# A text gate spread over its rows by eight transfers inside SBUF, in an image-and-text attention block on one core

## The chip, the cores and the metric

The kernel runs on one core of a Trainium2 chip. The metric is device time in microseconds (us) of one launch. Three runs of the kernel before took 117.28, 117.15 and 116.58 us, median 117.15. All positions in time below are from one profiled execution, counted from the start of its span.

Engine names are those of the profile: PE is TensorE's matmuls and PEld its weight loads, DVE is VectorE, ACT is ScalarE, POOL is GpSimd, SP is SyncE. SPq, ACTq and POOLq are the queues on which these engines issue DMA transfers.

## The reference

Two batches of 256 image tokens and 32 text tokens with 1152 features go through one block of joint attention. The part that matters is the end of it:

```python
mod_t = (_silu(c) @ wmod_txt).reshape(B, 6, 1, D)
...
sht, sct, gat = mod_t[:, 0], mod_t[:, 1], mod_t[:, 2]
...
a = softmax(q @ k.T * D ** -0.5) @ v          # text and image tokens together
at, ai = a[:, :Nt], a[:, Nt:]
out_i = x_img + gai * (ai @ wo_img)
out_t = x_txt + gat * (at @ wo_txt)
```

`gat` is the text gate: one row of 1152 numbers for each batch. Every one of a batch's 32 text rows of `at @ wo_txt` is multiplied by it, element by element, before `x_txt` is added. `gai` is the same for the image.

## The kernel before

The kernel is one long program for five engines with one order of instructions for each, written out by hand: the scheduler is set to manual, so an engine's instructions stand in the order in which the Python code emits them, and a wait at the head of an engine's queue holds everything behind it. Tiles come out of pools with a fixed number of buffers, used in turn; a tile that takes over a buffer waits for the last reader of the tile before it. PSUM has seven such buffers under one tag (`mm`), each one bank.

It loads 14 blocks of weights on SyncE's queue one after the other, and TensorE works through them: the image's modulation and V, then Q and K for the image (line 459), the text's Q and K (line 518), scores and softmax, the attention product (line 682), and last the output products. Only this last stage is touched by the change.

**Image output.** The 512 image rows are four tiles of 128; each tile's 1152 output columns are made in three chunks of 384 (`out_chunk`). A chunk is nine matmuls on TensorE (line 773), a VectorE multiply by the image gate out of PSUM (line 779) and a VectorE add of `x_img` (line 780). The last chunk of the last tile is cut into 256 and 128 columns; its weights are gated beforehand by GpSimd (line 757), so that VectorE only has to add (line 776). Tiles 0 to 2 are stored in one transfer each on SyncE's queue (line 784), tile 3 piece by piece, the piece of 256 columns on ScalarE's queue and the others on SyncE's (line 782).

**Text output.** The 64 text rows are few for 128 partitions, so the 1152 columns are laid out as two halves r of two groups g of 288 columns: text row t of batch b stands, for group g, in partition 64 g + 32 b + t, and half r is a second stretch along the row. `out_txt_mm` makes both halves in two PSUM tiles (`ops`) with 72 matmuls (line 794).

**Text gate.** `txt_gate` calls `mod_rows`: 36 matmuls (line 432) that leave in one PSUM tile `gps`, for quarter q = 2 r + g of the columns, batch b's gate in row 32 q + b. The tile is copied to SBUF as bf16 (`g_sb`, 288 columns) by `evac`, a helper that takes VectorE and ScalarE in turn and here takes VectorE (line 151). Only eight of its 128 rows hold gate values.

**Spreading.** Each text row needs its gate in its own partition. `txt_gate_spread` does that with two matmuls (line 747), one for each half r: the weights are `selF`, a 0/1 matrix that picks row 32 (2 r + g) + b for each of the 32 rows of (g, b); the result (`bps`) is copied by ScalarE to `gbf` (line 749). `selF` is made early, by eight small copies on GpSimd (line 333).

**Text end.** `out_txt_end` takes each half through a VectorE multiply by `gbf` (line 803) and an add of `x_txt` (line 804), then stores the two groups, one on SyncE's and one on ScalarE's queue (line 807).

The order in which these are emitted at the end is: tiles 0 and 1, tile 2's first two chunks, text gate, text products, spreading, text end, tile 2's last chunk, tile 3.

## Time and profile before

| What | Value |
|---|---|
| Median of three runs (lowest, highest) | 117.15 us (116.58, 117.28) |
| The profiled execution's own time | 116.77 us |
| Its span in the profile | 114.7 us |
| TensorE busy | 110.0 us, 96% |
| VectorE busy | 53.6 us, 47% |
| ScalarE busy | 34.1 us, 30% |
| GpSimd busy | 25.0 us, 22% |
| Granted TensorE clock | full in all 40 slices |

The span is the stretch from the first to the last instruction in the trace; the profiled execution's own time is 2.0 us longer. Busy shares are averages over stages with different limits, so what a change is worth is read from the stage in which it lies. The chain that ended last follows the work back from the last instruction, at each step to what released it. In a row of a group or of the timeline stand the line, the engine, the operation, the tile written and the tile read, the shapes, how many, and then busy time, mean length and what the engine waited for; matmul rows overlap, since they are pipelined, so the distance from one start to the next says more than the length of one. In the rows by half microseconds stand the stretch, its length, the busy time of PE, PEld, DVE, ACT and POOL with the number of instructions, the granted clock, the busy share of the DMA engines and GB/s. A row of a DMA issue names the transfer, its size, and the time from the start of its issue to its landing.

### The profile page before, as it was taken

How to read it: one execution, taken by the hardware profiler on the slowest of the kernel's cores; microseconds unless marked ns; L12 is line 12 of the kernel's file. 1: busy time of each engine (PE TensorE's matmuls, PEld its weight loads, DVE VectorE, ACT ScalarE, POOL GpSimd, SP SyncE). 2: the span in 40 equal slices, each digit the busy share in tenths (PEclk: the TensorE clock that was granted, in tenths of full speed). 3: DMA queues.
4: the chain of work that ended last, by engine and by line, in shares of the span. 5: the costliest groups of instructions: out<-in, count | busy, mean ns of one | idle time of the engine just before them, and what ended most of it. 6: DMA issues, size and time to landing. Idle time of an engine off the chain costs nothing.

```text
span 114.7 us, 2951 instructions
## 1 busy us (share of the span) xinstructions
PE 110.0 (96%) x1264; PEld 65.6 (57%) x1264; DVE 53.6 (47%) x139; ACT 34.1 (30%) x83; POOL 25.0 (22%) x56
## 2 busy tenths in 40 slices
PE   5998999999999999999999999999999999999990
PEld 1354664544944444486444546987677565567670
DVE  1798820452470402211752432137656805994771
ACT  2829660343360321021270122115455700000200
POOL 7000102560140000003233000000340301998000
PEclk9999999999999999999999999999999999999999
DMA  3999999999999999999999999999999999961052
GB/s 116 297 319 352 369 384 400 412 413 411 410 404 404 411 412 405 410 411 415 401 411 411 392 412 409 407 415 401 411 405 405 405 419 408 407 244 70 6 189 69
DMA packets 22872, 40.89 MB, mean 356 GB/s; under 512 B 1215, under 2 KB 6731, under 8 KB 22859
## 3 DMA queue, kind: packets, MB, share of 16 engines
q1 hardware_dynamic: 22000, 39.82, 91.0%
q0 software_dynamic: 480, 0.73, 1.7%
q10 hardware_dynamic: 379, 0.14, 0.5%
q8 instruction: 10, 0.16, 0.5%
q14 instruction: 3, 0.02, 0.1%
HBM read 39.36 MB, written 1.34 MB: 355 GB/s over the span
## 4 chain that ended last, share of the span: by engine, by line
PE 87%; DMA 6%; SPq 2%; DVE 2%; issue 0%
PE qkps L459 31%; PE ps L773 15%; PE va L242 11%; DMA x_i<-in_x_img_dram 6%; PE aps L682 5%; PE ps L518 4%; PE sps L542 4%; PE gps L370 4%; PE ops L794 2%; PE ps L346 2%; PE ps L397 2%; PE ps L614 2%; SPq L93 2%; PE mps L202 1%; PE gps L432 1%; PE tp L185 1%
## 5 line engine op out<-in xcount | busy, mean ns | idle before, releaser
L459 PE MATMUL qkps<-hT_i,t 128*128 128x512 bf16 x162 | 35.6, 379 | 0.0
L459 PEld LDWEIGHTS <-t 128*128 128x128 bf16 x162 | 15.6, 98 | 18.3
L773 PE MATMUL ps<-t,aT 128*128 128x384 bf16 x99 | 16.4, 326 | 0.0
L773 PEld LDWEIGHTS <-aT 128*128 128x128 bf16 x117 | 11.1, 98 | 6.7 <-issue 0.2
L242 PE MATMUL va<-w_v_i,hT_i 128*128 128x512 bf16 x63 | 14.5, 379 | 0.3 <-DMA w_v_i<-in_wqkv_img_dram 0.3
L757 POOL TENSOR_TENSOR w_og<-t,gb 128x384 bf16<-128x384 bf16 x9 | 8.7, 997 | 5.9 <-DMA t<-in_wo_txt_dram 5.9
L242 PEld LDWEIGHTS <-hT_i 128*128 128x128 bf16 x63 | 5.8, 97 | 7.0 <-ACT hT_i L190 0.6
L779 DVE TENSOR_TENSOR tmp<-ps,gb 128x384 bf16<-128x384 f32 x11 | 6.0, 549 | 4.8 <-DMA gb<-mod_scratch 4.0
L443 DVE TENSOR_SCALAR qkT<-qkps 128x512 bf16<-128x512 f32 x4 | 2.8, 692 | 11.6 <-PE qkps L459 11.6
L137 PE MATMUL wps<-wz 128*128 128x512 bf16 x16 | 6.2, 546 | 1.2 <-DVE wz L127 1.2
L160 DVE BATCH_NORM_STATS2 stats<-x_i 128x6 f32<-128x384 bf16 x12 | 5.9, 544 | 2.7 <-DMA x_i<-in_x_img_dram 2.7
L445 ACT ACTIVATE qkT<-qkps 128x512 bf16<-128x512 f32 x5 | 2.9, 596 | 13.5 <-PE qkps L459 13.5
L151 DVE CAST qkT<-qkps 128x512 bf16<-128x512 f32 x4 | 2.8, 692 | 7.2 <-PE qkps L459 7.2
L226 POOL TENSOR_SCALAR hT_i<-hT_i,mod_img 128x256 bf16<-128x256 bf16 x5 | 2.5, 510 | 15.7 <-ACT rstd L167 9.0
L153 ACT CAST qkT<-qkps 128x512 bf16<-128x512 f32 x5 | 2.8, 587 | 10.3 <-PE qkps L459 10.3
L569 POOL DMA_DIRECT2D mod_scratch<-g_sb x2 | 1.2, 583 | 20.9 <-ACT g_sb L567 20.9
L780 DVE TENSOR_TENSOR o<-tmp,x_i 128x384 bf16<-128x384 bf16 x11 | 5.2, 473 | 0.4
L695 DVE TENSOR_SCALAR aT<-aps,sv 128x288 bf16<-128x288 f32 (+2 forms) x11 | 4.3, 454 | 2.2 <-PE aps L682 2.2
L518 PEld LDWEIGHTS <-t 128*128 128x128 bf16 x162 | 4.9, 98 | 0.2
L749 ACT CAST gbf_full<-bps 128x288 bf16<-128x288 f32 x2 | 0.7, 402 | 14.2 <-PE bps L747 14.2
L518 PE MATMUL ps<-hT_t,t 128*128 128x64 bf16 x162 | 4.9, 193 | 0.0
L682 PE MATMUL aps<-pT,v_i 128*128 128x288 bf16 (+2 forms) x44 | 4.8, 264 | 0.1
(157 smaller groups left out, 141.2 us busy)
## 6 DMA issues: line engine op xcount, KB each, us to landing
t<-in_wmod_txt_dram SPq DMA_DIRECT2D x3, 2592.0 KB, 22.0
t<-in_wmod_img_dram SPq DMA_DIRECT2D x2, 2592.0 KB, 22.4
t<-in_wqkv_img_dram SPq DMA_DIRECT2D x6, 864.0 KB, 14.1
t<-in_wqkv_txt_dram SPq DMA_DIRECT2D x2, 2592.0 KB, 17.4
t<-in_wqkv_txt_dram SPq DMA_DIRECT2D x3, 864.0 KB, 14.2
t<-in_wo_img_dram SPq DMA_DIRECT2D x1, 2592.0 KB
t<-in_wo_txt_dram SPq DMA_DIRECT2D x3, 864.0 KB, 15.0
w_v_i<-in_wqkv_img_dram SPq DMA_DIRECT2D x4, 576.0 KB, 7.8
```

The lines of the kernel that those rows point to most:

```text
L137: nc.tensor.matmul(ps[:], lhsT=wz[:, 0:P], rhs=wz[:], start=True, stop=True)
L160: nc.vector.bn_stats(stats[0:np_, k, :], x_ap[:, k * CH:(k + 1) * CH])
L242: nc.tensor.matmul(ps[:], lhsT=hT_i[:, kt, i * P:(i + 1) * P], rhs=w_v_i[:, kt, half * VW:(half + 1) * VW], start=(kt == 0), stop=(kt == K ...
L370: nc.tensor.matmul(gps[32 * g:32 * g + 32, 0:RC], lhsT=lhs[:, kt, :], rhs=wt[:, kt, g * RC:(g + 1) * RC], start=(kt == 0), stop=(kt == KT ...
L459: nc.tensor.matmul(pss[j - j0][:], lhsT=wq[:, kt, j * P:(j + 1) * P], rhs=hT_i[:, kt, :], start=(kt == 0), stop=(kt == KT - 1))
L518: nc.tensor.matmul(ps[:, j - j0, :], lhsT=wq[:, kt, j * P:(j + 1) * P], rhs=hT_t[:, kt, :], start=(kt == 0), stop=(kt == KT - 1))
L542: nc.tensor.matmul(sps[:], lhsT=qkT[:, ft, b, q0:q0 + P], rhs=qkT[:, KT + ft, b, :], start=(ft == 0), stop=(ft == KT - 1))
L682: nc.tensor.matmul(bank[:, off:off + c1 - c0], lhsT=lhsT, rhs=rhs, start=(first[id(bank)] == n), stop=(final[id(bank)] == n))
L757: nc.gpsimd.tensor_mul(w_og[:, dt, 0:CH], w_o_i[:, dt, NG0:D], gb[:, B - 1, NG0:D])
L773: nc.tensor.matmul(ps[:, 0:cw], lhsT=aT[:, dt, t0:t0 + P], rhs=rhs, start=(dt == DTS[0]), stop=(dt == DTS[-1]))
L779: nc.vector.tensor_mul(tmp[:, 0:cw], ps[:, 0:cw], gb[:, b, cs])
L780: nc.vector.tensor_add(o[:, cs], tmp[:, 0:cw], x_i[:, i, cs])
```

## The change

The selection matrix `selF` and its eight GpSimd copies go. `mod_rows` copies the gate rows to SBUF on ScalarE, by name, where `evac` chose VectorE. The spreading is done without TensorE and ScalarE's copies: for each batch b, half r and group g, one transfer reads row 32 (2 r + g) + b of `g_sb` 32 times and writes the 32 partitions from 64 g + 32 b on of `gbf`. The four transfers of batch 0 are issued on SyncE's queue, those of batch 1 on ScalarE's. And the order at the end is another: the spreading is issued right behind the gate products and ahead of the text products, and the text end stands behind tile 2's last chunk instead of ahead of it. The text products, the text end's own instructions and all image chunks are the same.

```diff
-    selF = const.tile([P, 2, 2, B, NT], bf)
-    for r in range(2):
-        for g in range(2):
-            for b in range(B):
-                col = 32 * (2 * r + g) + b
-                nc.gpsimd.tensor_copy(selF[:, r, g, b, :], ident[:, col:col + 1].to_broadcast([P, NT]))
...
-        evac(g_sb[:, 0:VC], gps[:])
+        nc.scalar.copy(g_sb[:, 0:VC], gps[:])
...
     def txt_gate_spread(g_sb):
-        for r in range(2):
-            bps = ps_mm.tile([P, VC], f32, tag="mm")
-            nc.tensor.matmul(bps[:], lhsT=selF[:, r, :, :, :].rearrange("p g b t -> p (g b t)"), rhs=g_sb[:, 0:VC],
-                             start=True, stop=True)
-            nc.scalar.copy(gbf[:, r, :], bps[:])
+        for b in range(B):
+            eng = nc.sync if b == 0 else nc.scalar
+            for r in range(2):
+                for g in range(2):
+                    row = 32 * (2 * r + g) + b
+                    q = 64 * g + NT * b
+                    eng.dma_start(gbf[q:q + NT, r, :], g_sb[row:row + 1, 0:VC].rearrange("p (o j) -> p o j", o=1).to_broadcast([1, NT, VC]))
...
     g_sb = txt_gate()
+    txt_gate_spread(g_sb)
     pss = out_txt_mm()
-    txt_gate_spread(g_sb)
+    out_chunk(2, 2 * CH, CH)
     out_txt_end(pss)
-    out_chunk(2, 2 * CH, CH)
     out_chunk(3, 0, CH, nc.sync)
```

## The prediction

> **What bounds the kernel now.** I read the page first (busy shares, the 40 slices), then the chain that ended last, then the timelines of TensorE and VectorE from 95 us on, last the busy time and the DMA share by half microseconds.

> ```profile
> PE 110.0 (96%) x1264; PEld 65.6 (57%) x1264; DVE 53.6 (47%) x139; ACT 34.1 (30%) x83; POOL 25.0 (22%) x56
> ...
> PE 87%; DMA 6%; SPq 2%; DVE 2%; issue 0%
> ```

> TensorE is busy 96% of the span, and 87% of the chain that ended last is its matmuls. Until about 101 us the weight loads fill the DMA engines too, but the change lies behind them. The chain in order of time, around the change (start, length, what):

> ```profile
> 102.36 1.22 PE gps L432 x36
> 103.58 2.21 PE ops L794 x72
> 105.78 0.35 PE bps L747 x2
> 106.14 5.89 PE ps L773 x45
> 112.02 0.02 issue
> 112.05 0.29 DVE o L776
> ```

> No step here waits for another engine: gate products, text products, the two selection products, then the 45 matmuls of the last five chunks. Only the final VectorE add stands behind them, then store and closing. So time is saved only by taking work off TensorE, and lost only by what comes later than 112.05. VectorE at that end:

> ```profile
> 106.48 0.46 DVE L803 TENSOR_TENSOR tmp<-ops,gbf_full 128x288 bf16<-128x288 f32 x1 [2.02 <-ACT gbf_full L749]
> 106.97 0.31 DVE L804 TENSOR_TENSOR of<-tmp,xf_full 128x288 bf16<-128x288 bf16 x1
> 107.20 0.45 DVE L803 TENSOR_TENSOR tmp<-ops,gbf_full 128x288 bf16<-128x288 f32 x1
> 107.69 0.31 DVE L804 TENSOR_TENSOR of<-tmp,xf_full 128x288 bf16<-128x288 bf16 x1
> 107.91 0.55 DVE L779 TENSOR_TENSOR tmp<-ps,gb 128x384 bf16<-128x384 f32 x1
> 108.50 0.36 DVE L780 TENSOR_TENSOR o<-tmp,x_i 128x384 bf16<-128x384 bf16 x1
> 109.10 0.56 DVE L779 TENSOR_TENSOR tmp<-ps,gb 128x384 bf16<-128x384 f32 x1 [0.24 <-PE ps L773]
> 109.69 0.36 DVE L780 TENSOR_TENSOR o<-tmp,x_i 128x384 bf16<-128x384 bf16 x1
> 110.56 0.56 DVE L779 TENSOR_TENSOR tmp<-ps,gb 128x384 bf16<-128x384 f32 x1 [0.51 <-PE ps L773]
> ```

> The text end (four instructions, 106.48 to 107.91, 1.43 us) runs while TensorE makes tile 2's last chunk, so VectorE has caught up by 109.10 and again by 110.56, with gaps of 0.24 and 0.51 us. That slack, 0.75 us and what is left behind 110.56, is what a later text end uses up.

> **TensorE: two products of 128x288 go.** The chain puts 0.35 us on them. But the weight load in front of them shows a gap of 0.24 us (the arrays change from 32 columns to 128), which the chunk behind will have instead. In the TensorE timeline the first selection product starts at 105.72 and the first matmul of the chunk at 105.97:

> ```profile
> 105.72 0.42 PE L747 MATMUL bps<-g_sb,selF 128*128 128x288 bf16 x2
> 105.97 4.55 PE L773 MATMUL ps<-t,aT 128*128 128x384 bf16 x27
> ```

> So the chunks come 0.25 us earlier (0.35 at most, if the gap goes as well). I take 0.25. TensorE gets no new wait: the spread is off it, and of the seven banks used in turn the chunks get ones read before 104.1.

> **GpSimd: eight copies go**, 1.25 us from 22.2 us on. GpSimd then idles 5.7 us for a VectorE result (line 224), so this is worth nothing.

> **The gate copy goes from VectorE to ScalarE.** VectorE took it at 104.02, between chunks; ScalarE has waited 14.2 us by line 749 and does this shape in 402 ns. Gate products end at 103.58, so the row tile is ready at about 104.02, against 104.47.

> **Eight transfers come**, four from SyncE's queue, four from ScalarE's, each reading one row of 576 bytes 32 times. This trace has none like it. On SyncE they stand behind tile 1's store (issued 102.14) and before tile 2's, which has no data before 108.2; on ScalarE before a text store and the store of a last piece, later still. Each takes over the completion counter of the eighth transfer before it; for the last two those are tiles 0's and 1's stores, and the DMA engines carry nothing from 104.5 on, so neither should hold them. The bus is free:

> ```profile
> 104.50:105.00 0.50, 0.50 (x25) 0.43 (x16) 0.00 (x0) 0.00 (x0) 0.50 (x2) 1.00 0.00 0
> 105.00:105.50 0.50, 0.50 (x28) 0.43 (x16) 0.00 (x0) 0.00 (x0) 0.50 (x1) 1.00 0.00 0
> ```

> The nearest rows are the text stores (the same 576-byte pieces, both queues, an idle bus) and the last small store:

> ```profile
> out_dram<-of SPq DMA_DIRECT2D x1, 72.0 KB, 2.2
> out_dram<-of ACTq DMA_DIRECT2D x1, 72.0 KB, 2.5
> ...
> out_dram<-o SPq DMA_DIRECT2D x1, 32.0 KB, 1.5
> ```

> Issuing took 0.61 to 0.65 us in the text stores, 0.33 in the 32 KB one; with some 0.06 between, one every 0.4 to 0.7 us. From 104.05 the second on each queue (half r=0 complete) starts at 104.45 to 104.75, the fourth (r=1) at 105.25 to 106.15. With 1.5 to 2.5 us to landing: r=0 is there at 105.95 to 107.25, r=1 at 106.75 to 108.65. I take the text stores' row: 107.2 and 108.5.

> **The text end moves behind tile 2's last chunk.** In before the next chunk is taken at 109.10 and the one after at 110.56, 1.46 us apart at TensorE's pace, so tile 2's last chunk was ready at 107.64 and is now at 107.39. A chunk on a VectorE with work waiting takes 0.87 us to the next (95.86 to 96.73, GpSimd idle; 0.98 while GpSimd gates weights, over by 105.7; 0.95 if nothing overlaps). So:
> - chunk 107.39 to 108.26; the text end's first half needs r=0 at 108.26, its second r=1 at 108.98 (0.72 later, as 106.48 to 107.20); both are there, by 1.0 and 0.5 us;
> - text end to 109.69, tile 3's chunks to 110.56 and 111.43 (ready on TensorE at 108.85 and 110.31, so VectorE now sets the pace);
> - the 256 columns: ready 111.29, taken 111.43, 0.42 us at most; the last 128: ready about 111.8, end 112.1.

> Before ended at 112.34. So VectorE just works off its backlog as TensorE ends, and the 0.25 us arrives at the end. With 0.95 a chunk the sum is 112.4: no gain. The two text stores move from 108.02 to 109.7, still 2 us ahead of the last. The four waits in front of the text multiply cost a few hundredths, beside the running add.

> **The sum.** The profiled execution took 116.77 us (span 114.7, 2.0 around it): 116.77 - 0.25 = 116.5. The runs' median is 117.15, 0.4 above it; by that 116.9.

> **Rivals.**

> 1. *The source rows are the bottleneck (slower).* All 147 KB come out of eight rows of SBUF, where every store of this trace reads 64 or 128. If rows lying together give no more than a sixteenth of the full rate (410 GB/s in the slices, so 25.6), the 74 KB of r=0 take 2.9 us: 104.05 + 1.5 + 2.9 = 108.45, 0.2 late. If r=1 goes abreast from 105.0, it lands at about 109.4, 0.4 late: 117.3. If each DMA engine must finish r=0 first, r=1 lands at 111.35, 2.4 late: VectorE stands still and the end moves by 2.4 - 0.25: 119.3. It decides from a landing at 109.2 (gain gone); by 110.4 the kernel is 1% slower. For it: eight rows only. Against it: nothing in the trace reads so few rows at this size.

>    [...]

> 2. *VectorE becomes the bound, transfers hidden.* With 0.95 to 0.98 us a chunk and small costs for waits the end is 112.4 to 112.5: 117.2 to 117.3. For it: five of the seven steps between earlier chunks take 0.98. Against: those run beside GpSimd.

> 3. *The products' removal shows nothing or more.* If TensorE's array change costs more before the wider chunk, the gain is 0; if the gap goes too, 0.35: 116.8 to 117.15. Nothing in the diff can give over 1%, since only 0.35 us leaves the path.

> **How the numbers follow.** Hidden transfers, 116.8 to 117.3 (the forecast, rivals 2 and 3): 0.50. Source rows limiting, halves mostly abreast, 117.3 to 118.3: 0.24. The same in sequence, 118.3 to 119.3: 0.23. Faster by over 1%, only by an effect I do not see: 0.03. One per cent, 1.17 us, is about what a measurement of this kernel can tell from no change; so faster 0.03, same 0.74, slower 0.23. The range runs from 116.5 (forecast less the runs' own scatter of 0.4) to 119.0, leaving the worst of rival 1 out.

> **What would show it.** Right: no selection products, the chunk's first matmul within 0.3 us of the last text product; eight transfers issued from 104.1, landing by 108.5; VectorE without a gap from 107.4 on. Wrong: a wait on a transfer of the gate tile ahead of a text multiply (rival 1; its length is the loss); gaps on VectorE behind the text end would say that I priced the chunks too high.

## The result, and the profile after

The changed kernel took 118.78 us (median of 6 runs, 118.51 to 119.0), beside 117.02 us for the kernel before (also 6 runs). The ratio is 1.0147, with a 95% interval of 1.0122 to 1.0172: **slower by 1.5%**, where the prediction had 116.9 us and no change. Its profiled execution took 118.59 us, with a span of 116.8.

Line numbers of the changed kernel are five to seven lower than before: the transfers are on L744, the chunks on L768, L774 and L775, the text end on L798 and L799. From the page, the busy shares and the shares of the chain:

```profile
PE 109.7 (94%) x1262; PEld 65.3 (56%) x1262; DVE 52.9 (45%) x138; ACT 33.9 (29%) x82; POOL 23.8 (20%) x48
...
PE 79%; DVE 9%; DMA 6%; ACTq 2%; issue 1%; ACT 0%; DVEq 0%
```

The work is smaller on every engine, and the time is longer: 2.1 us of span were added, and TensorE does nothing in them. Its share of the chain that ended last fell from 87% to 79%, and VectorE's rose from 2% to 9%. The chain in order of time shows where TensorE drops out:

```profile
102.42 1.25 PE gps L425 x36
103.67 0.02 issue
103.69 0.41 ACT g_sb L428
104.10 0.02 issue
104.12 0.60 ACTq L744
...
106.33 4.39 DMA gbf_full<-g_sb
...
110.85 0.47 DVE tmp L798
```

In before the products stood in this place without a break. Now the chain leaves TensorE at 103.67, goes through the gate copy and the four issues on ScalarE's queue, and then spends 4.39 us on the last of these transfers. The prediction had that step hidden. VectorE's timeline (start, length, engine, line, operation, shapes, and in brackets what it waited for) says how late it is:

```profile
107.45 0.56 DVE L774 TENSOR_TENSOR tmp<-ps,gb 128x384 bf16<-128x384 f32 x1 [3.25 <-PE ps L768]
108.04 0.36 DVE L775 TENSOR_TENSOR o<-tmp,x_i 128x384 bf16<-128x384 bf16 x1
108.62 0.46 DVE L798 TENSOR_TENSOR tmp<-ops,gbf_full 128x288 bf16<-128x288 f32 x1 [0.22 <-DMA gbf_full<-g_sb]
109.11 0.31 DVE L799 TENSOR_TENSOR of<-tmp,xf_full 128x288 bf16<-128x288 bf16 x1
110.85 0.46 DVE L798 TENSOR_TENSOR tmp<-ops,gbf_full 128x288 bf16<-128x288 f32 x1 [1.43 <-DMA gbf_full<-g_sb]
111.34 0.31 DVE L799 TENSOR_TENSOR of<-tmp,xf_full 128x288 bf16<-128x288 bf16 x1
111.56 0.55 DVE L774 TENSOR_TENSOR tmp<-ps,gb 128x384 bf16<-128x384 f32 x1
...
112.42 0.55 DVE L774 TENSOR_TENSOR tmp<-ps,gb 128x384 bf16<-128x384 f32 x1
...
113.28 0.61 DVE L771 TENSOR_TENSOR o<-ps,x_i 128x256 bf16<-128x256 f32 x2
```

The first text multiply waits 0.22 us for half r=0, the second 1.43 us for half r=1. Behind the second wait stand tile 3's chunks, which TensorE had ready long before (it ends at 111.82), so the last add ends at 113.90. The stage's start differs a little between profiles, since the first loads do; so from here on the end is given as **tail**: the end of the last VectorE add, counted from the first gate product. These are the rows of the first gate product and the last adds in before, and of the first gate product in after:

```profile
102.29 1.29 PE L432 MATMUL gps<-t,sT 128*32 128x288 bf16 x36
111.54 0.80 DVE L776 TENSOR_TENSOR o<-ps,x_i 128x256 bf16<-128x256 f32 x2
```

```profile
102.35 1.29 PE L425 MATMUL gps<-t,sT 128*32 128x288 bf16 x36
```

Before, the tail is 112.34 - 102.29 = 10.05 us; after, it is 113.90 - 102.35 = 11.55.

TensorE itself did what was foreseen. By its timeline the chunk behind the text products starts 3.42 us after the first gate product (105.77 - 102.35), where it was 3.68 in before (105.97 - 102.29):

```profile
103.46 2.38 PE L789 MATMUL ops<-t,aT 128*32 128x288 bf16 x72
105.77 4.56 PE L768 MATMUL ps<-t,aT 128*128 128x384 bf16 x27
```

The transfers, by the rows of DMA issues (queue, size of one, median time from issue to landing) and by half microseconds (the last two columns are the busy share of the DMA engines and GB/s):

```profile
gbf_full<-g_sb SPq DMA_DIRECT2D x4, 18.0 KB, 3.5
gbf_full<-g_sb ACTq DMA_DIRECT2D x4, 18.0 KB, 3.9
out_dram<-of SPq DMA_DIRECT2D x1, 72.0 KB, 2.1
```

```profile
105.50:106.00 0.50, 0.50 (x14) 0.20 (x7) 0.00 (x0) 0.00 (x0) 0.34 (x1) 1.00 0.31 28
106.00:106.50 0.50, 0.50 (x5) 0.31 (x4) 0.00 (x0) 0.00 (x0) 0.00 (x0) 1.00 0.62 28
106.50:107.00 0.50, 0.50 (x5) 0.31 (x4) 0.00 (x0) 0.00 (x0) 0.00 (x0) 1.00 0.74 29
107.00:107.50 0.50, 0.50 (x5) 0.31 (x4) 0.05 (x1) 0.00 (x0) 0.00 (x0) 1.00 0.71 28
107.50:108.00 0.50, 0.50 (x5) 0.30 (x4) 0.50 (x1) 0.00 (x0) 0.00 (x0) 1.00 0.67 65
```

A transfer of 18 KB takes longer to land than a text store of 72 KB. From 105.5 to 107.5, while only half r=0 is read, the DMA engines are up to 74% busy and move 28 GB/s. In the packet records of the trace a 576-byte piece takes mostly 0.21 to 0.25 us from 106 on (median 0.23); pieces of that size took 0.03 to 0.04 us in the text stores. Only when pieces of r=1, which read other rows, come among those of r=0 does the rate double to 65 GB/s.

**A second loss** lies behind the last landing. It takes 0.91 us from there to the end of the span in before (113.83 to 114.74) and 1.28 in after (115.52 to 116.80); this is called the closing below. The tail's 1.50 us and the closing's 0.37 make 1.87, against 1.72 by the ratio (0.0147 of 117.05, interval 1.43 to 2.01).

### The profile page after: what moved, and what is told of

Read it like the earlier page. It is cut to its first block, busy times and chain, and to the rows that moved or that the text cites. A ratio compares the mean times of both kernels' runs of the same rounds, so it can differ in the third digit from the quotient of the medians.

```text
span 116.8 us, 2950 instructions
## 1 busy us (share of the span) xinstructions
PE 109.7 (94%) x1262; PEld 65.3 (56%) x1262; DVE 52.9 (45%) x138; ACT 33.9 (29%) x82; POOL 23.8 (20%) x48
## 4 chain that ended last, share of the span: by engine, by line
PE 79%; DVE 9%; DMA 6%; ACTq 2%; issue 1%; ACT 0%; DVEq 0%
PE qkps L452 30%; PE va L242 10%; PE ps L768 10%; PE aps L675 5%; PE ps L511 4%; DVE stats L160 4%; PE sps L535 4%; DMA gbf_full<-g_sb 4%; PE gps L363 4%; DMA x_i<-in_x_img_dram 3%; PE ps L339 2%; ACTq L744 2%; PE ps L390 2%; PE ps L607 2%; DVE xn_i L172 1%; PE mps L202 1%
## 5 line engine op out<-in xcount | busy, mean ns | idle before, releaser
L768 PE MATMUL ps<-t,aT 128*128 128x384 bf16 x99 | 16.4, 326 | 0.0
L768 PEld LDWEIGHTS <-aT 128*128 128x128 bf16 x117 | 11.0, 98 | 6.8 <-issue 0.5
L774 DVE TENSOR_TENSOR tmp<-ps,gb 128x384 bf16<-128x384 f32 x11 | 6.0, 548 | 7.3 <-DMA gb<-mod_scratch 4.1
L775 DVE TENSOR_TENSOR o<-tmp,x_i 128x384 bf16<-128x384 bf16 x11 | 5.2, 471 | 0.4
L690 ACT ACTIVATE aT<-aps,sv 128x288 bf16<-128x288 f32 (+2 forms) x11 | 4.0, 468 | 2.2 <-PE aps L675 2.2
```

Of the source, the lines that this page charges most:

```text
L768: nc.tensor.matmul(ps[:, 0:cw], lhsT=aT[:, dt, t0:t0 + P], rhs=rhs, start=(dt == DTS[0]), stop=(dt == DTS[-1]))
L774: nc.vector.tensor_mul(tmp[:, 0:cw], ps[:, 0:cw], gb[:, b, cs])
L775: nc.vector.tensor_add(o[:, cs], tmp[:, 0:cw], x_i[:, i, cs])
```

## The experiments

Five questions were asked: is it the rows that are read; what are the other parts of the change worth; does a spreading by few transfers gain what was forecast; what lengthens the closing; and what made one experiment slow for a reason of its own. In the expectations letters stand for theories, and a "door" is a way out of SBUF that several rows are supposed to share; what held is said in words behind each. Two measures go with each kernel, the tail and the closing, each from one profiled execution, beside its ratio to before. A ratio compares with runs of before on the same chip; the chip changed from one group of experiments to the next, so ratios can be compared and times cannot.

### Is it the rows that are read?

**The two halves on different queues.** The theory is that the eight rows are the limit and that r=1 waits for r=0 because both stand in the same two queues. Here half r=0 goes through SyncE's queue and r=1 through ScalarE's, so that both sets of rows are read at once.

```diff
-            eng = nc.sync if b == 0 else nc.scalar
             for r in range(2):
+                eng = nc.sync if r == 0 else nc.scalar
```

> The changed kernel with one thing altered: the four transfers of half r=0 go on SyncE's queue and those of r=1 on ScalarE's, where each queue had one batch. Same rows, same bytes, same count. Theory A (rows lying together in SBUF share a door of about 28 GB/s, and a queue works through its transfers in order, so r=1 stood behind r=0): the two doors are now read from the start, 74 KB at 28 GB/s is 2.6 us for both halves side by side, all eight land by 108.3 to 108.8 instead of 110.7, VectorE waits at most 0.4 us, and the time is 116.9 to 117.3, level with the kernel before. Theory B (a transfer inside SBUF is slow for each DMA engine, 0.22 us for 576 bytes whichever rows it reads): nothing changes, last landing about 110.7, time 118.8.

Measured: 118.47 us, ratio 1.0135 (1.0105 to 1.0166), tail 11.42. The rate doubled as foreseen, to 53 to 55 GB/s from 106.5 to 108.0, pieces took 0.06 to 0.07 us, and the median landing came 2.3 us after issue on one queue and 2.5 on the other. But the time hardly moved, where 116.9 to 117.3 had been expected of theory A. VectorE's timeline of this run:

```profile
108.74 0.36 DVE L775 TENSOR_TENSOR o<-tmp,x_i 128x384 bf16<-128x384 bf16 x1
110.70 0.46 DVE L798 TENSOR_TENSOR tmp<-ops,gbf_full 128x288 bf16<-128x288 f32 x1 [1.61 <-DMA gbf_full<-g_sb]
111.20 0.31 DVE L799 TENSOR_TENSOR of<-tmp,xf_full 128x288 bf16<-128x288 bf16 x1
111.42 0.45 DVE L798 TENSOR_TENSOR tmp<-ops,gbf_full 128x288 bf16<-128x288 f32 x1
```

Now the first multiply waits 1.61 us and the second not at all. By the landing records each half had arrived on all DMA engines but one by 109.12 and 109.34; the last one reported at 110.68 and 110.85. In this stretch one 16 KB packet of q8, the queue that the page calls "instruction", was under way from 108.32 to 109.62 (taken here for a load of program text), and the last text-gate pieces start from 109.60 on. The trace does not name the DMA engine of a packet, so that it was the same one is read from these times and not shown. In the changed kernel such a load runs from 108.54 to 109.49 and the last landings are at 110.55 and 110.72, while the other engines are done by 110.18: by these times some 0.55 of its 1.43 us are of this kind.

**More rows.** The gate product is given sixteen copies of each batch's column, which costs TensorE nothing (its weights are 32 columns wide anyway, and the 36 products take 1.29 us in this run as in after), so that 16 rows hold each gate row and each is read twice instead of 32 times.

```diff
+        for m in range(16):
+            nc.gpsimd.tensor_copy(sTw[:, :, B * m:B * (m + 1)], sT[:])
...
-                nc.tensor.matmul(gps[32 * g:32 * g + 32, :], lhsT=sT32[:, kt, :], ...
+                nc.tensor.matmul(gps[32 * g:32 * g + 32, :], lhsT=sTw[:, kt, :], ...
...
-                    eng.dma_start(gbf[q:q + NT, r, :], g_sb[row:row + 1, 0:VC]....to_broadcast([1, NT, VC]))
+                    eng.dma_start(gbf[q:q + NT, r, :], g_sb[row:row + 31:2, 0:VC]....to_broadcast([16, 2, VC]))
```

> The changed kernel, but the gate products leave each gate row 16 times (the 32 columns of their weights hold the two batches in turn, 16 times, instead of two columns and 30 zeros; the number and shape of the matmuls is the same), and each of the eight transfers reads 16 different rows twice instead of one row 32 times. Queues, order and bytes as in the changed kernel. Theory A: no door is crowded any more, a packet takes 0.03 to 0.08 us as in the text stores, transfers land 2.2 to 2.5 us after their issue, the last by 108.8; VectorE does not wait; 116.7 to 117.1. Theory B: packets stay at 0.22 us, last landing about 110.7, 118.8.

Measured: 121.53 us, ratio 1.0398 (1.037 to 1.0425). The pieces went down to 0.030 us, as the theory said, but the kernel was slower from its first loads on: the gate stage began at 105.58. This run therefore decides nothing on the time; the reason is taken up below (the new tile `sTw` has 576 bytes a partition, and it moved the tiles behind it). The same spreading was run again with the tile padded to 1024 bytes, one GpSimd copy making all sixteen, and eight more copies on GpSimd that nobody reads, so that its program is about as long as in before:

```diff
-    sTw = const.tile([P, KT, 32], bf)
+    sTw_full = const.tile([P, 512], bf)
+    sTw = sTw_full[:, 0:32 * KT].rearrange("p (k c) -> p k c", c=32)
...
+    for n in range(8):
+        nc.gpsimd.tensor_copy(sTw_full[:, 32 * KT:32 * KT + 32], ident[:, n:n + 1].to_broadcast([P, 32]))
```

> Again the changed kernel with each gate row left 16 times and eight transfers that read 16 rows twice, on the same queues and in the same order, but the added tile of weights is padded to 1024 bytes so that no later tile moves off its place, one GpSimd copy fills it, and eight small GpSimd copies of no use stand where the selection matrix was made. Theory A and E: loads at 410 GB/s, packets of the gate at 0.03 us, the last of the eight lands some 2.4 us after its issue, 0.2 us or more before the text end's second half, VectorE runs without a gap, the last add stands 9.80 us behind the first gate product (10.05 in the kernel before), closing 0.91 us: 116.7 to 116.95, ratio about 0.998. If each transfer inside SBUF were slow whatever the rows: 11.5 and 118.7.

Measured: 117.64 us, ratio 1.0031 (1.0002 to 1.0061), tail 10.39, closing 0.92. The pieces take 0.030 us, the loads are back at 410 GB/s, and more than a full microsecond of the loss is gone though the eight transfers and their bytes are the same. The tail of 9.80 that was expected did not come, for one wait is left:

```profile
108.48 0.45 DVE L804 TENSOR_TENSOR tmp<-ops,gbf_full 128x288 bf16<-128x288 f32 x1
...
109.86 0.46 DVE L804 TENSOR_TENSOR tmp<-ops,gbf_full 128x288 bf16<-128x288 f32 x1 [0.58 <-DMA gbf_full<-g_sb]
```

Fifteen of the last transfer's sixteen landing reports came by 108.40, the sixteenth at 109.74; a program load ran from 107.40 to 108.39 and the late pieces start at 108.39. With the 0.58 us gone the tail would be 9.81.

**Which rows.** Rows alone, or what neighbouring rows share? Batch 1's gate is put into row 4 of each group of 32 instead of row 1. The number of rows and of readings of each stays. The weights for it stand in a padded tile whose filling takes three more GpSimd instructions than the changed kernel has; `selF` is not made.

```diff
+    sTw_full = const.tile([P, 512], bf)
+    sTw = sTw_full[:, 0:32 * KT].rearrange("p (k c) -> p k c", c=32)
...
+    nc.gpsimd.memset(sTw[:], 0.0)
...
+        for b in range(B):
+            nc.gpsimd.tensor_copy(sTw[:, :, 4 * b:4 * b + 1], sT[:, :, b:b + 1])
...
-                    row = 32 * (2 * r + g) + b
+                    row = 32 * (2 * r + g) + 4 * b
```

> The changed kernel with batch 1's gate row left in row 4 of each group of 32 instead of row 1 (its weights in a padded tile, loads in place); still eight transfers, each reading one row 32 times, same queues and order. [...] If a door is the whole lower half of the rows, nothing changes: 28 GB/s, 11.5 us, 118.7.

Measured: 117.72 us, ratio 1.004 (1.0013 to 1.0066), tail 10.43, closing 0.91. The half microseconds in which only r=0 is read:

```profile
106.50:107.00 0.50, 0.50 (x7) 0.31 (x4) 0.00 (x0) 0.00 (x0) 0.23 (x1) 1.00 0.44 54
107.00:107.50 0.50, 0.50 (x5) 0.29 (x3) 0.00 (x0) 0.00 (x0) 0.00 (x0) 1.00 0.46 59
```

### What the other parts are worth

**No spreading at all.** The transfers are left out and `gbf` is filled with ones early, so the text output lacks its gate; everything else is the changed kernel. This measures the change with transfers that are perfectly hidden.

```diff
+    nc.gpsimd.memset(gbf_full[:], 1.0)
...
-                    eng.dma_start(gbf[q:q + NT, r, :], ...)
```

> The changed kernel without the eight transfers: the tile of spread gates is filled with ones by GpSimd long before, so the text output lacks its gate. It shows what the rest of the change is worth when nothing has to land. Theory A: the whole loss is the landing, so VectorE runs from tile 2's last chunk to the end without a gap and the last add ends 0.2 to 0.3 us earlier than in the kernel before: 116.7 to 116.9. Theory C (the loss lies in the text end's new place, VectorE's backlog behind it): the last add ends 0.5 us or more after that of before, 117.5 or more.

Measured: 117.35 us, ratio 1.003 (1.0011 to 1.0049), tail 9.80, closing 1.40. The tail is shorter by exactly the 0.25 us that the prediction took off TensorE, and VectorE works without a gap from 107.94 to the end, at 0.86 us a chunk. The time is nevertheless a little longer, where 116.7 to 116.9 had been expected: by the trace the closing, 0.49 longer, takes the gain and more.

**The text end moved, alone,** in the kernel before; and **not moved,** in the changed one.

```diff
     pss = out_txt_mm()
...
+    out_chunk(2, 2 * CH, CH)
     out_txt_end(pss)
-    out_chunk(2, 2 * CH, CH)
```

> The kernel before with only the text end moved behind tile 2's last chunk; the gate still spreads by two products with the selection matrix. Theory A: VectorE has room for the later text end, so the time stays within 0.2 us of the kernel before, 116.9 to 117.2. Theory C: VectorE becomes the bound by the move alone, 117.5 or more.

> The changed kernel with the text end left where it was, ahead of tile 2's last chunk; the eight transfers as in the changed kernel. VectorE then waits with nothing in between from 104.2 until r=0 is there (108.4) and again until r=1 is (110.7), and three chunks instead of two stand behind the text end: the last add moves by one more chunk, 0.87 us, against the changed kernel, 12.4 us behind the first gate product, time 119.5 to 119.8. If the landing were not what the end hangs on, the place would not matter: 118.8.

Measured: moved alone, 116.91 us, ratio 0.9994 (0.9973 to 1.0016), tail 10.05 as before. So the move costs nothing. Not moved in the changed kernel: 119.7 us, ratio 1.0199 (1.0156 to 1.0242), tail 12.40. Without it all of the text end's waiting stands in front of one more chunk, and the loss is 0.85 us of tail larger than with it (4.42 and 1.39 us of waits, text multiplies at 108.97 and 111.16). The move is the part of the change that helps; it hides some of this landing, and not all of it.

### The same with two transfers

64 rows hold each half of the gate (16 copies of each gate row, side by side), and each half is one transfer that reads its 64 rows twice. The tile is padded, and eight copies on GpSimd that nobody reads keep its instruction count near that of before. The second kernel has the text end ahead of the last chunk again.

```diff
+        for b in range(B):
+            nc.gpsimd.tensor_copy(sTw[:, :, 16 * b:16 * (b + 1)], sT[:, :, b:b + 1].to_broadcast([P, KT, 16]))
...
-        for b in range(B):
-            ...
+        for r in range(2):
+            eng = nc.sync if r == 0 else nc.scalar
+            eng.dma_start(gbf[:, r, :], g_sb[64 * r:64 * r + 64, 0:VC]....to_broadcast([64, 2, VC]))
```

> The changed kernel with two transfers in place of eight. The 32 weight columns of the gate products hold batch 0 sixteen times and then batch 1 sixteen times, so 64 rows of the gate tile hold each half r, and one transfer per half reads each of 64 rows twice and writes all 128 partitions; r=0 on SyncE's queue, r=1 on ScalarE's. The weights lie in a tile padded to 1024 bytes, so that all later tiles keep their place modulo 512 bytes, and GpSimd does eight small copies of no use where the selection matrix was made. Theory A (crowded rows, and pieces waiting behind one another): both land 2.2 to 2.6 us after an issue some 0.5 us behind the gate products, over a microsecond before the text end; packets of 576 bytes at 0.03 to 0.05 us; VectorE without a gap; the last add 0.25 us earlier than in the kernel before, time 116.7 to 116.9. If transfers inside SBUF were slow as such (0.2 us for a packet whatever the rows), they would land some 4 us after issue and VectorE would wait: 117.3 or more.

> As the kernel with two transfers, but the text end stands ahead of tile 2's last chunk, as in the kernel before. Theory A: the transfers land about 0.7 us before that chunk is ready, the text end overlaps its matmuls, VectorE has its gaps back and the end hangs on TensorE alone: 116.7 to 116.9, the same as with the text end behind the chunk. If the landing is later than 2.9 us after issue, the text end pushes the chunks back and this one is 0.2 to 0.5 us slower than the other.

Measured: 117.04 us, ratio 1.0009 (0.9992 to 1.0026), and 117.11 us, 1.0004 (0.9984 to 1.0024). Both tails are 9.80 and both closings 1.27. In the first kernel the transfers are issued at 104.64 and land 2.1 and 2.4 us later, and VectorE has no wait for them. In the second they take as long; VectorE waits for them with nothing else to do, and has caught up with TensorE by tile 3's chunks, which it waits for again, as in before:

```profile
107.28 0.46 DVE L801 TENSOR_TENSOR tmp<-ops,gbf_full 128x288 bf16<-128x288 f32 x1 [2.28 <-DMA gbf_full<-g_sb]
...
109.87 0.56 DVE L777 TENSOR_TENSOR tmp<-ps,gb 128x384 bf16<-128x384 f32 x1 [0.22 <-PE ps L771]
...
111.34 0.56 DVE L777 TENSOR_TENSOR tmp<-ps,gb 128x384 bf16<-128x384 f32 x1 [0.51 <-PE ps L771]
```

So the spreading by transfers can be hidden entirely, and the 2.2 and 2.5 us of the text stores, which the prediction took, are right for a transfer that reads 64 rows. Both also landed some 0.7 us before the program load of these kernels began (107.04 against 107.75 in the first), and no part of them was late. The 0.25 us arrive at the last add. In the time, for which 116.7 to 116.9 had been expected, they do not show.

### What lengthens the closing

In the kernels with 72 or 73 GpSimd instructions (after has 72) the records behind the last landing show a stall of some 0.4 us on GpSimd before it clears its semaphores (in after from 115.96 to 116.36); in kernels with 75 or more (before has 80) there is none. In the two-transfer kernels that stall is absent, and SyncE is late instead: at the end it goes through nine checks one after the other, eight of them of the transfers' completion counters, at some 0.06 us each. Where the counter of the last store, on which it has to wait, is in the third check of that row, six checks follow behind the wait; in before it is in the last. Transfers on the two queues take eight counters in turn (numbers 100, 102, 103 and 105 to 109 in the trace of before), so the number of transfers decides which one the last store gets; eight more transfers change nothing, two more do.

**The copies kept.** The changed kernel with `selF` and its copies left in, though nothing reads them:

```diff
+    selF = const.tile([P, 2, 2, B, NT], bf)
+    ...
+                nc.gpsimd.tensor_copy(selF[:, r, g, b, :], ident[:, col:col + 1].to_broadcast([P, NT]))
```

> The changed kernel with the selection matrix and its eight GpSimd copies still made, though nothing reads it. Theory D: the closing of the program on GpSimd stalls by 0.35 to 0.5 us wherever these eight instructions are missing (from last landing to the end of the span: 1.28 us in the changed kernel and with the halves side by side, 1.40 without transfers, against 0.91 in the kernel before, with the text end moved alone, and with 16 copies added at the start). With the copies back the closing takes 0.91 us and the time falls from 118.8 to 118.4. If the eight copies are as free as the prediction priced them, the time stays at 118.8 and the closing at 1.28.

Measured: closing 0.91, as expected of it, but 118.76 us, where 118.4 was expected; the ratio of 1.0141 (1.0115 to 1.0166) is hardly below after's. The tail was 11.67, 0.12 longer than in after, by a later landing. The sum of both is 0.25 less than after's, which lies within the two intervals; the run shows the closing's cause and not its price.

**Two tiny transfers** of 64 bytes each are added to the kernel before, out of a weight block, behind the attention product, into a tile that nobody reads:

```diff
+    tiny = small.tile([16, 2, 2], bf, bufs=1)
+    for n in range(2):
+        nc.scalar.dma_start(tiny[:, n, :], wmod_img[0:P:8, 2 * n:2 * n + 2])
```

> The kernel before with two transfers of 64 bytes added on ScalarE's queue in its idle stretch before the output products; nothing reads them. The completion counters of transfers go round in eights, and at the end SyncE checks them in a fixed order, 0.06 us each. Theory F: the last store then has a counter that is checked third and not last, six more checks follow its landing, and the closing grows from 0.91 to about 1.27 us as in both kernels with two transfers for the gate: 117.3 to 117.5, ratio 1.003. If the closing there had another cause, it stays at 0.91 and the time at 117.05.

Measured: closing 1.27 and tail 10.05, both as expected; 117.44 us against 117.2, ratio 1.001 (0.9985 to 1.0034). So the number of transfers does lengthen the closing, and that it does so through the counters is read from the order of SyncE's checks. In the time both 0.36 us and zero lie within the interval, so how much of it is paid stays open here.

**Two transfers and six tiny ones:** the kernel of two transfers, text end behind the chunk, and six of the tiny ones, eight more than before in all: the gain of 0.25 us with the closing of before.

```diff
...
+    tiny = small.tile([16, 6, 2], bf, bufs=1)
+    for n in range(6):
+        nc.scalar.dma_start(tiny[:, n, :], wmod_img[0:P:8, 2 * n:2 * n + 2])
```

> The two transfers of 64 rows, each row read twice (gate products and rows as in the earlier run of two transfers), and six transfers of 64 bytes each out of a weight block, behind the attention product, into a tile that nobody reads: with the two they make eight more transfers than in the kernel before, so that every completion counter is taken as often as by the changed kernel and the last store's counter stands where it stood before. If the closing is a matter of which counter the last store uses, it is 0.91 us again and not 1.27; the last add stays at 9.80 us behind the first gate product (10.05 before). Sum theory (the 0.25 us taken off TensorE and the closing are all there is): ratio 0.998, about 116.9. Rival (what is seen at the closing in the trace is not in the time): the time stays where the run of two transfers had it, ratio 1.001, although the closing is back at 0.91.

Measured: tail 9.80, closing 0.90, and 116.87 us against 117.23, ratio 0.999 (0.9966 to 1.0014). The closing is back, as foreseen. Of the two ratios expected, 0.998 is the nearer, but both lie in the interval, so it stays open whether the 0.25 us reach the time. Its ratio is the lowest of the kernels here, by less than the noise: it is not measurably faster than before, nor than before with the text end moved (0.9994).

All kernels whose loads were not slowed, on one scale. The last two columns are the tail and closing together less before's (10.96), and the ratio less one times 117.1:

| Kernel | Tail | Closing | Sum of changes, us | By the ratio, us |
|---|---|---|---|---|
| before | 10.05 | 0.91 | 0 | 0 |
| after | 11.55 | 1.28 | +1.87 | +1.72 |
| halves abreast | 11.42 | 1.27 | +1.73 | +1.58 |
| 16 rows, padded | 10.39 | 0.92 | +0.35 | +0.36 |
| rows 0 and 4 | 10.43 | 0.91 | +0.38 | +0.47 |
| no spreading | 9.80 | 1.40 | +0.24 | +0.35 |
| before, text end moved | 10.05 | 0.90 | -0.01 | -0.07 |
| after, text end not moved | 12.40 | 1.29 | +2.73 | +2.33 |
| two transfers | 9.80 | 1.27 | +0.11 | +0.11 |
| two transfers, text end ahead | 9.80 | 1.27 | +0.11 | +0.05 |
| after, copies kept | 11.67 | 0.91 | +1.62 | +1.65 |
| before, two tiny transfers | 10.05 | 1.27 | +0.36 | +0.12 |
| two transfers and six tiny ones | 9.80 | 0.90 | -0.26 | -0.12 |

The two columns agree within the intervals (0.2 to 0.5 us to either side), so nothing large is missing from this account.

### Why the sixteen-row kernel was slow everywhere

The theory: its new tile of 576 bytes a partition moved the tiles behind it in SBUF to places where loads are slower. To test it alone, the kernel before got one unused tile of 64 bytes a partition, and nothing else:

```diff
+    shim = const.tile([P, 32], bf)
+    nc.gpsimd.memset(shim[:], 0.0)
     eps_t = const.tile([P, 1], f32)
```

> The kernel before with one added tile of 64 bytes per partition, cleared once by GpSimd and used by nothing, which moves every later tile of SBUF by 64 bytes. Theory E: the kernel with 16 copies of each gate row was slow at its loads (2304-byte packets 100 ns instead of 94, 390 GB/s instead of 410) because its added tile of 576 bytes moved the weight tiles off their places; this kernel then shows the same packets and 390 GB/s and takes 118.5 to 121. If instead the sixteen added copies on GpSimd or something else of that kernel was at fault, this one stays at 117.0.

Measured: 121.44 us, ratio 1.0378 (1.0348 to 1.0409). The ten microseconds from 50 us on, in which the weight loads fill the DMA engines, first of before and then of this kernel (the last two figures of a row are the DMA engines' busy share and GB/s):

```profile
50.00:60.00 10.00, 10.00 (x153) 6.03 (x146) 4.71 (x15) 3.28 (x6) 2.32 (x5) 1.00 1.04 408
```

```profile
50.00:60.00 10.00, 9.95 (x165) 6.19 (x165) 3.12 (x9) 1.66 (x4) 1.61 (x3) 1.00 1.05 391
```

391 GB/s where it was 408, with the engines as busy: the sixteen-row kernel has 391 as well. So that kernel's 4% were the shift, and not its spreading, which the padded run then bore out.

## Why the prediction was wrong

The step that failed is the landing of the eight transfers. The prediction took it from the text stores, "the nearest rows", and had r=0 there at 107.2 and r=1 at 108.5, ahead of need by 1.0 and 0.5 us. Measured, r=0 was there at 108.43 and the last of r=1 at 110.72. The issues were nearly as foreseen (104.11 to 106.33 at 0.58 to 0.84 us each, where 0.4 to 0.7 was taken). It was the reading: 28 GB/s out of four rows (0, 1, 32 and 33), not the stores' rate; and the transfers of r=1 stood behind those of r=0 in both queues. The text stores share the size of the pieces, the queues and the idle bus, but each of them reads 64 rows, and the number and place of the rows was what counted. The prediction saw this, wrote it as its first rival with a price, and gave it 0.47 against 0.50 for hidden transfers; what it held against it was that "nothing in the trace reads so few rows".

- **Rival 1, in sequence,** is what happened: it put r=0 0.2 us late and r=1 2.4 us late, landing at 111.35, and the time at 119.3. Measured: 0.22 and 1.43 us of waits, 110.72, and 118.78. The rate (25.6 GB/s supposed, a sixteenth of the full rate, which no row of before shows; 28 measured) was nearly right. r=1 was less late, because its pieces run beside the end of r=0's from 107.5 on, although some 0.55 us of its wait seem to come from the program load. That the time is so near to this rival's is partly luck: 0.37 us of the loss are the longer closing, which the rival does not have.
- **Rival 1, abreast** (117.3) was run by itself and came to 118.47. The rows were read at the double rate, but one late part in sixteen of each half cost 1.61 us; this delay, by the times that of a program load, is in none of the prediction's cases.
- **TensorE, 0.25 us:** right, to the hundredth in every kernel whose end does not wait for the gate (tail 9.80 against 10.05).
- **The eight GpSimd copies, "worth nothing":** right where they stood, wrong at the end. Without them the closing is 0.37 us longer, and with them kept it is not. Why the stall hangs on the number of GpSimd instructions stays open: no packet of a program load shows in that stretch of the traces.
- **The gate copy on ScalarE:** right. It ended at 104.09, where 104.02 was foreseen and the stage began 0.06 later.
- **VectorE's chain, 0.87 us a chunk, and no gap behind the text end:** right. Its steps are 0.86 (111.56, 112.42, 113.28), so rival 2 with 0.95 is out, and the move of the text end is free by its own run. The four waits in front of the text multiply, put at a few hundredths, cost nothing that shows where the transfers were in time: the first one starts 0.28 us behind the start of the chunk's add with rows 0 and 4 (108.78 to 109.06), and 0.28 without any transfer (108.53 to 108.81).
- **The sum:** even with hidden transfers, the sum would have been too low: without any spreading the time was 0.35 us above before's, with two transfers 0.11, where 0.25 below was forecast (the interval is clear of no change in the first, and not in the second). The 0.25 us come to the last add, and by the table the longer closing takes them back. That would still have been no change within 1%.

## What to carry to other kernels

Price a transfer that reads SBUF by the rows it reads and where they lie, not by its bytes: four rows (0, 1, 32 and 33) gave 28 GB/s here, and moving half of them by three rows, or making copies in a product whose columns were idle, took most of the loss away. A rival that has a price should not be discounted because the trace has no such row; ask first what the row put in its place does not share with the new operation. And a transfer needed within 2 or 3 us should have more slack than its own length, since one of its sixteen parts may come late by up to 1.6 us, as here beside a program load of about 1 us.

## What the runs showed of the hardware that was not expected

- An unused tile of 64 bytes a partition made the whole kernel 3.8% slower, by moving the tiles behind it. Pieces of 2304 bytes took 99.6 ns on average instead of 94.3, and those of 512 bytes 30.1 instead of 27.5. What about the new places made the loads slower is not shown by any run.
- The queue that the page calls "instruction" (q8, 10 packets, 0.16 MB) moves packets of 16 KB, taken here for loads of program text. In every kernel here one starts 4.7 to 6.3 us behind the first gate product and takes 0.95 to 1.35 us. In all six kernels with eight transfers in place and the loads not slowed, it falls among the gate's pieces; the pieces that start as it ends were the last to land, and the part of the last transfer that they belong to came 0.5 to 1.5 us after the other fifteen. It cost VectorE up to 1.61 us.
- The closing depends on things that have no part in the computation: two transfers of 64 bytes behind the attention product moved it from 0.91 to 1.27 us.
